# K cache transposed on VectorE in 32x32 blocks of 4-byte pairs, in a decode kernel that streams its K and V caches

## The chip, the cores and the metric

The kernel runs on one core of a Trainium2 chip. The time is device microseconds (us) of one execution. The time before is 392.98 us (median of 3 runs, 392.82 to 393.05). On one core there are no two dies to compare, so a run counts as slow only if it lies over 1.5% above the fastest of the same kernel; a profiled run's own span is about 2 us shorter than its time. The "granted clock" in the tables is the share of TensorE's full clock that the profile records as granted.

The engines are called TensorE (PE in the profile, PEld for its weight loads), VectorE (DVE), ScalarE (ACT), GpSimd (POOL) and SyncE (SP), which issues the loads. Sixteen DMA engines share each load: through the long loads 16 packets are under way at a time, and each large load has 16 landings in the trace.

## The reference, cut to what matters

One token (x is 1x1024) goes through grouped-query attention over a cache of 65536 positions, and through a small gated MLP. A gate mixes the two.

```python
# Hq, Hkv, Sk, Dh = 32, 4, 65536, 128 ; D = 1024 ; bf16
q = (x @ wq)                                   # wq 1024 x 4096
scores = q . k_cache * Dh**-0.5                # 8 query heads share a kv head
o = softmax(scores) . v_cache
a = o @ wo                                     # wo 4096 x 1024
# B: z = gelu(x @ w_in); z1 * (w_sp * layernorm(z2) + b_sp) @ w_out, one row
return g * a + (1 - g) * b                     # g = sigmoid(sum(x * gate_w))
```

K and V take 67.1 MB each (4 x 65536 x 128 values of 2 bytes), and with the weights the kernel reads 162.0 MB, all of it once.

## The kernel before: the parts that matter

Every large load takes one of `NKV` buffers of 32 KB per partition from one ring, in program order on SyncE's queue. A load waits until the buffer used `NKV` loads earlier has been read for the last time.

```python
NKV = 5
kv = ctx.enter_context(tc.tile_pool(name="kv", bufs=NKV))
def load(src, shape, name):
    t = kv.tile([P, CT * P], BF16, name=name, tag="kv")
    ...
    nc.sync.dma_start(out=v, in_=src)
```

The order of the loads is: two halves of w_in, two of wq, the four K tiles of kv head (group) 0, then K and V in turn (K of group g, V of group g-1), the four V tiles of group 3, w_out, and wo in six pieces. A K or V tile is 128 positions for each of 128 partitions: 4.19 MB.

A K tile has positions on partitions, but the scores contract over the head dimension. So TensorE transposes K in 128x128 pieces, VectorE and ScalarE take turns to copy the result out of PSUM, and TensorE multiplies each piece (as weights) by q:

```python
def k_units(g, j, kn):
    for u in range(CT // TG):
        tps = pst.tile([P, TG * P], BF16, name="tps")
        for i in range(TG):
            nc.tensor.transpose(tps[:, i * P:(i + 1) * P], kn[:, u * TG + i, :], ident_b[:])
        ktt = ktp.tile([P, TG * P], BF16, name="ktt")
        if EVAC_PAT[evac_i[0] % len(EVAC_PAT)] == "a":
            nc.scalar.copy(out=ktt[:], in_=tps[:])
        else:
            nc.vector.tensor_copy(out=ktt[:], in_=tps[:])
        ...
def emit_scores(g, cg0, ktt):
    ...
    for j in range(TG):
        ...
        nc.tensor.matmul(spt[g][:, o:o + n], lhsT=ktt[:, j * P:(j + 1) * P],
                         rhs=qT[:, g * REP:g * REP + n], start=True, stop=True, ...)
```

The work on V is interleaved with the work on the next group's K. When a group's scores are complete, its maximum is found, the exps are taken and the V matmuls begin. Each of these three jobs is cut into small steps.

## Time and profile before

| | before |
|---|---|
| time | 392.98 us |
| bytes loaded | 162.0 MB |
| DMA share, 60 to 366 us | 100% |
| instructions | 11536 |
| instruction bytes fetched (queue q8) | 0.69 MB in 42 packets of 16 KB |

The page of the kernel before: busy time by engine, then the DMA share in tenths and the GB/s for 40 equal slices of the span (9.8 us each), two DMA queues, and the shares of the chain of waits.

```profile
PE 289.8 (74%) x5355; PEld 240.1 (61%) x5355; DVE 160.2 (41%) x316; ACT 122.2 (31%) x139; POOL 1.0 (0%) x9
...
DMA  8999999999999999999999999999999999999982
GB/s 332 426 434 432 431 432 430 424 427 432 429 425 424 426 432 438 429 427 427 424 434 431 427 431 423 427 431 431 428 431 431 427 429 425 436 427 419 432 348 100
...
q1 hardware_dynamic: 6200, 162.01, 96.9%
q8 instruction: 42, 0.69, 0.7%
...
DMA 55%; PE 39%; issue 2%; DVE 2%; ACT 1%; SPq 0%; DVEq 0%; ACTq 0%
```

TensorE looks busiest, and the chain of waits gives it 39%, but the DMA rows show what binds: the loads never pause between the first slice and the last two. The kernel takes as long as its bytes take. Only the ends (332, 348 and 100 GB/s) leave room.

The groups that the change is about (line, engine, operation, tiles, shapes, count | busy us, mean ns | idle before):

```profile
L328 PE MATMUL tps<-ident_b,kn 128*128 128x128 bf16 x2048 | 163.6, 225 | 36.5 <-DMA kn<-in_A_k_cache_dram 34.9
L333 DVE COPY ktt<-tps 128x1024 bf16<-128x1024 bf16 x171 | 116.4, 689 | 111.9 <-PE tps L328 111.2
L331 ACT COPY ktt<-tps 128x1024 bf16<-128x1024 bf16 x85 | 86.0, 1012 | 161.5 <-PE tps L328 161.4
L307 PE MATMUL spt<-qT,ktt 128*128 128x64 bf16 (+7 forms) x2048 | 104.0, 194 | 5.3 <-issue 5.3
```

The table by stretch shows the tail. Its columns are the stretch, its length, the busy us (and instructions) of PE, PEld, DVE, ACT and POOL, the granted clock, the DMA share and GB/s. (A DMA packet is counted whole in the stretch in which it starts, so in a short stretch the share can pass 1.)

```profile
374.00:378.00 4.00, 0.16 (x4) 0.13 (x7) 0.00 (x0) 0.00 (x0) 0.00 (x0) 0.50 0.95 392
378.00:382.00 4.00, 3.44 (x64) 2.66 (x57) 0.00 (x0) 0.00 (x0) 0.00 (x0) 0.50 0.57 241
382.00:386.00 4.00, 2.75 (x48) 2.01 (x48) 0.00 (x0) 0.00 (x0) 0.00 (x0) 0.50 0.46 187
```

Between 378 and 386 us only about half of the 16 DMA engines still work, although everything had been queued since 349 us.

### The profile page before, as it was taken

To read this page: it belongs to the slowest core of one execution; us is meant where nothing else is said; L and a number is where in the kernel's file an instruction comes from. 1 tells how busy PE (TensorE), PEld (TensorE's weight loads), DVE (VectorE), ACT (ScalarE), POOL (GpSimd) and SP (SyncE) were. 2 spreads that over 40 slices of the span, in tenths; PEclk is the share of its full clock that TensorE was granted. 3 is DMA by queue.
4 is the path that set the end of the run, shared out by engine and by line. 5 is a ranking of instruction groups with operands and counts; after the bars stand their busy time and mean duration, and the time that the engine had idled before them with its cause. 6 is when DMAs were issued, how large, how long until landed. Compare 5 with 4: busy or idle time off the path is not lost.

```text
span 391.0 us, 11536 instructions
## 1 busy us (share of the span) xinstructions
PE 289.8 (74%) x5355; PEld 240.1 (61%) x5355; DVE 160.2 (41%) x316; ACT 122.2 (31%) x139; POOL 1.0 (0%) x9
## 2 busy tenths in 40 slices
PE   0774379888899995969994979589959697634534
PEld 0764379888887774846873858368848583311322
DVE  3011036665684551518750526177524356200200
ACT  1000025454594432413831434136414243100000
POOL 1000000000000000000000000000000000000000
PEclk9999999999999998989996999898989998866656
DMA  8999999999999999999999999999999999999982
GB/s 332 426 434 432 431 432 430 424 427 432 429 425 424 426 432 438 429 427 427 424 434 431 427 431 423 427 431 431 428 431 431 427 429 425 436 427 419 432 348 100
DMA packets 6285, 162.76 MB, mean 416 GB/s; under 512 B 728, under 2 KB 732, under 8 KB 1116
## 3 DMA queue, kind: packets, MB, share of 16 engines
q1 hardware_dynamic: 6200, 162.01, 96.9%
q8 instruction: 42, 0.69, 0.7%
q14 instruction: 7, 0.06, 0.0%
q10 hardware_dynamic: 36, 0.00, 0.0%
HBM read 162.01 MB, written 0.00 MB: 414 GB/s over the span
## 4 chain that ended last, share of the span: by engine, by line
DMA 55%; PE 39%; issue 2%; DVE 2%; ACT 1%; SPq 0%; DVEq 0%; ACTq 0%
DMA kn<-in_A_k_cache_dram 38%; PE tps L328 23%; PE spt L307 10%; DMA wo_t<-in_A_wo_dram 10%; DMA vt<-in_A_v_cache_dram 6%; PE o_ps L353 5%; DVE ktt L333 1%; ACT ktt L331 1%; PE s_ps L361 0%; PE om_ps L371 0%; SPq L84 0%; ACT scT L313 0%; DVE scT L290 0%; PE nb_ps L285 0%; PE mxT L277 0%
## 5 line engine op out<-in xcount | busy, mean ns | idle before, releaser
L328 PE MATMUL tps<-ident_b,kn 128*128 128x128 bf16 x2048 | 163.6, 225 | 36.5 <-DMA kn<-in_A_k_cache_dram 34.9
L333 DVE COPY ktt<-tps 128x1024 bf16<-128x1024 bf16 x171 | 116.4, 689 | 111.9 <-PE tps L328 111.2
L328 PEld LDWEIGHTS <-kn 128*128 128x128 bf16 x2048 | 123.7, 101 | 62.2 <-DMA kn<-in_A_k_cache_dram 38.5
L331 ACT COPY ktt<-tps 128x1024 bf16<-128x1024 bf16 x85 | 86.0, 1012 | 161.5 <-PE tps L328 161.4
L307 PE MATMUL spt<-qT,ktt 128*128 128x64 bf16 (+7 forms) x2048 | 104.0, 194 | 5.3 <-issue 5.3
L307 PEld LDWEIGHTS <-ktt 128*128 128x128 bf16 x2048 | 86.7, 100 | 7.0 <-issue 6.7
L353 PE MATMUL o_ps<-vt,scT 128*32 128x512 bf16 x512 | 54.2, 449 | 16.2 <-DMA vt<-in_A_v_cache_dram 15.4
L353 PEld LDWEIGHTS <-scT 128*32 128x32 bf16 x512 | 15.8, 103 | 29.3 <-issue 24.4
L313 ACT CAST scT<-spt 128x512 bf16<-128x512 f32 x32 | 18.8, 588 | 17.0 <-PE spt L307 17.0
L315 DVE TENSOR_TENSOR mxr<-scT,mxr 128x512 bf16<-128x512 bf16 x24 | 10.2, 426 | 20.1 <-ACT scT L313 18.8
L294 ACT ACTIVATE scT<-scT 128x1024 bf16<-128x1024 bf16 x16 | 16.4, 1059 | 5.1 <-DVE scT L290 5.1
L430 PE MATMUL out_ps<-wo_t,oa 128*32 128x256 bf16 x128 | 7.5, 399 | 10.4 <-DMA wo_t<-in_A_wo_dram 10.4
L192 PE MATMUL z_ps<-xT,win_t 128*128 128x18 bf16 x224 | 13.7, 208 | 1.6 <-DMA win_t<-in_B_w_in_dram 1.1
L192 PEld LDWEIGHTS <-win_t 128*128 128x128 bf16 x224 | 13.7, 158 | 1.6 <-DMA win_t<-in_B_w_in_dram 1.2
L368 DVE COPY o_sb<-o_ps 128x512 f32<-128x512 f32 x4 | 2.7, 687 | 28.0 <-PE o_ps L353 28.0
L361 PE MATMUL s_ps<-scT,ones_b 128*32 128x512 bf16 x32 | 13.4, 418 | 0.0
L430 PEld LDWEIGHTS <-oa 128*32 128x32 bf16 x128 | 5.3, 135 | 12.8 <-issue 12.0
L244 PE MATMUL q_ps<-xT,wq_t 128*128 128x1 bf16 x256 | 7.1, 165 | 7.6 <-DMA wq_t<-in_A_wq_dram 7.6
L244 PEld LDWEIGHTS <-wq_t 128*128 128x128 bf16 x256 | 7.0, 104 | 7.8 <-DMA wq_t<-in_A_wq_dram 7.8
L290 DVE TENSOR_TENSOR scT<-scT,negm 128x1024 bf16<-128x1024 bf16 x16 | 10.7, 683 | 0.2
L450 DVE CAST out_sb<-out_ps 128x256 bf16<-128x256 f32 x1 | 0.4, 424 | 22.6 <-PE out_ps L430 22.6
L371 PE MATMUL om_ps<-o_sb,pick 128*32 128x128 f32 x32 | 5.0, 310 | 3.2 <-DVE o_sb L368 3.2
(87 smaller groups left out, 51.4 us busy)
## 6 DMA issues: line engine op xcount, KB each, us to landing
kn<-in_A_k_cache_dram SPq DMA_DIRECT2D x16, 4096.0 KB, 30.0
vt<-in_A_v_cache_dram SPq DMA_DIRECT2D x16, 4096.0 KB, 31.3
wq_t<-in_A_wq_dram SPq DMA_DIRECT2D x2, 4096.0 KB, 30.1
win_t<-in_B_w_in_dram SPq DMA_DIRECT2D x2, 3584.0 KB, 15.2
wo_t<-in_A_wo_dram SPq DMA_DIRECT2D x1, 4096.0 KB, 42.7
wout_t<-in_B_w_out_dram SPq DMA_DIRECT2D x1, 3584.0 KB
wo_t<-in_A_wo_dram SPq DMA_DIRECT2D x1, 2048.0 KB
wo_t<-in_A_wo_dram SPq DMA_DIRECT2D x1, 1024.0 KB
```

Source lines behind the costliest of these rows:

```text
L192: nc.tensor.matmul(z_ps[:, hf * FC + f, :], lhsT=w[:, hf, f, :], rhs=xT[:, i * KH + c:i * KH + c + 1].to_broadcast([P, zw]), start=(i == 0 ...
L244: nc.tensor.matmul(q_ps[:, h:h + 1], lhsT=w[:, c % KH, h * DH:(h + 1) * DH], rhs=xT[:, c:c + 1], start=(c == 0 and h == 0), stop=(c == KC ...
L290: nc.vector.tensor_tensor(out=blk, in0=blk, in1=negm[:].unsqueeze(1).to_broadcast([P, CT, REP]), op=ALU.add)
L294: nc.scalar.activation(out=blk, in_=blk, func=ACT.Exp, scale=SCALE)
L307: nc.tensor.matmul(spt[g][:, o:o + n], lhsT=ktt[:, j * P:(j + 1) * P], rhs=qT[:, g * REP:g * REP + n], start=True, stop=True, skip_group_c ...
L313: nc.scalar.copy(out=blk, in_=spt[g][:].rearrange("p (c h) -> p c h", h=REP))
L328: nc.tensor.transpose(tps[:, i * P:(i + 1) * P], kn[:, u * TG + i, :], ident_b[:])
L331: nc.scalar.copy(out=ktt[:], in_=tps[:])
L333: nc.vector.tensor_copy(out=ktt[:], in_=tps[:])
L353: nc.tensor.matmul(o_ps[g][t * Q:(t + 1) * Q, :], lhsT=scT[g][:, cg:cg + VC, :].rearrange("p c h -> p (c h)"), rhs=vt[:, lo:lo + VC, :].re ...
L361: nc.tensor.matmul(s_ps[g][gs, :], lhsT=ones_b[:, :Q], rhs=scT[g][:, cg:cg + CPS, :].rearrange("p c h -> p (c h)"), start=(cg == 0), stop= ...
L430: nc.tensor.matmul(out_ps[t * Q:(t + 1) * Q, :], lhsT=vec[:, c0 + c:c0 + c + 1].to_broadcast([P, Q]), rhs=w[:, c, t * NO:(t + 1) * NO], st ...
```

## The change

The intent is to take the K transpose off TensorE and its copies off VectorE and ScalarE. VectorE transposes K with the bf16 data viewed as 4-byte pairs: one instruction takes 2048 pairs for each partition, two values per element. The kernel's indexing takes the result as 32x32 blocks (`B = 32`; the trace records shapes, not blocks). In that layout only 32 pairs lie on the partitions of each block row, so the weights hold q in a block-diagonal arrangement, and the 512-column moving operand is read at a step of 4 bytes. TensorE now has 32 wide score matmuls for a K tile in place of 128 transposes and 128 narrow ones. The x projections are computed as rows (x as 32 equal weight columns, 448 or 512 columns of weights moving). The new tables take room, so `NKV` goes from 5 to 4.

```diff
-NKV = 5
+NKV = 4
 ...
+    def k_tile(g, j, kn):
+        kb = kn.bitcast(I32)
+        n = CC * DH // 2
+        s_ps = pss.tile([P, 2 * HN], FP32, name="s_ps", tag="s")
+        for v in range(VC):
+            kt = ktp.tile([P, CC * DH], BF16, name="kt")
+            nc.vector.transpose(out=kt[:].bitcast(I32), in_=kb[:, v * n:(v + 1) * n])
+            kx = kt[:].rearrange("p (c h k e) -> p h e c k", h=2, k=B, e=2)
+            for b in range(BP):
+                for k in range(2):
+                    nc.tensor.matmul(
+                        s_ps[:, k * HN:(k + 1) * HN],
+                        lhsT=wt[g % 2][:, v, b].rearrange("p a v h -> p (a v h)"),
+                        rhs=kx[:, b // 2, b % 2, k * CC // 2:(k + 1) * CC // 2, :],
+                        start=(v == 0 and b == 0), stop=(v == VC - 1 and b == BP - 1), ...)
+        ...
+        nc.scalar.copy(out=sct[g, j][:], in_=s_ps[:])
+        nc.vector.reduce_max(out=mxs[g][:, j:j + 1], in_=sct[g, j][:], axis=AX.X)
 ...   (stats: group maximum; then for each of the group's 4 tiles)
+            nc.scalar.activation(out=sct[g, j][:], in_=sct[g, j][:], func=ACT.Exp, scale=SCALE,
+                                 bias=nb[:, 0:1], accum_out=lss[g][:, j:j + 1])
+            nc.vector.transpose(out=ptt[g, j][:]..., in_=sct[g, j][:])
 ...
+    for g in range(G):
+        for j in range(NT):
+            k_tile(g, j, load_kv(A_k_cache, g, j, "kn"))
+            if j == 1 and g + 1 < G:
+                build_w(g + 1)
+            if j == NT - 1:
+                stats(g)
+            if g > 0:
+                v_tile(g - 1, j, load_kv(A_v_cache, g - 1, j, "vt"))
 ...
```

## The prediction

> **What bounds it now.** Loads. The page moves 162.0 MB; in the table by stretch, the 16 DMA engines are 100% busy from 60 to 366 us at 427 to 429 GB/s, so one 4.19 MB tile takes about 9.75 us. 162.0 MB at 429 GB/s is already 378 us; start and tail add the other 13 us. TensorE (74%), VectorE (41%) and ScalarE (31%) have slack. The chain of waits names TensorE lines, but only as who frees buffers; with five buffers that never empties the queue. No byte of input is removed, so the gain is capped. The tail is unchanged: the last wo pieces are waited for by TensorE (7.8+1.3+0.5+... us).
>
> **What goes.** 2048 TensorE transposes (163.6 us busy), 256 evictions (116.4 us VectorE, 86.0 us ScalarE), 2048 score matmuls with own weights (104 us). All off the critical path. 11536 instructions become roughly 3500 (count from the diff); their fetching (0.69 MB, 0.7% of the DMA share) shrinks by two thirds: estimate 1 to 2 us saved.
>
> **What comes.** 64 VectorE transposes of 2048 4-byte elements. The trace has none; its [...]shapes (512-column f32 copy 687 ns, 128-column reduce 382 ns) give about 0.15 us + 1.04 ns each[...]: estimate 2.29 us, 9.2 us a K tile (no run shows it yet). 512 score matmuls of 512 columns, about 0.22 us warm, 0.43 us at half clock (four V matmuls of 512 columns in parallel take 0.22/0.43 us in the timeline): 7 us a tile. V work unchanged.
>
> **The catch.** VectorE is in program order, and after a tile's fourth transpose it must wait for the last eight matmuls (1.9 us), ScalarE's copy (1.0) and do reduce_max over 1024 columns (1.2) before the next tile's transposes. So a K tile costs VectorE about 13.5 us, against 9.75 us of loading. When K and V alternate (19.5 us a pair) that is free. In the first group four K tiles come back to back: transposes end at about 60, 74, 88, 102 us; then group statistics with four exps and four P transposes hold VectorE to about 114 us, and K tile (1,0) is released only at about 124 us. With four buffers instead of five, the load of K (1,2) waits for that release, while the queue runs dry at about 119 us. Estimated gap: 6 us, once (0 to 10). Later groups have about 64 us of VectorE work in 78 us of loading: no gap. With five buffers it would not occur.
>
> **Sum.** 393 - 1.5 + 6 = 397 us. Range 390 to 406. Faster by over 2%: 0.03; within 2%: 0.77; slower by over 2%: 0.20.
>
> **Right if:** mean of the transpose group near 2.3 us; TensorE busy falls below 200 us and ScalarE below 60; DMA share 100% except one hole around 115 to 128 us, at the first statistics, with the queue's own wait naming the VectorE transpose of K (1,0); instruction bytes about 0.25 MB; same tail.
>
> **Wrong if:** the 4-byte transpose runs at half rate (4.4 us): a K tile then costs 22 us, VectorE bounds everything and the time passes 450 us. Or TensorE stays at half clock, which lengthens the wait before reduce_max and the hole. Or transposes are quicker, or the scheduling leaves the hole closed: then about 391 us, the same as before. Reading the moving operand at a 4-byte step might slow the matmuls; up to about double is hidden except in group 0.

Two passages about the transposes are cut out of the text above. They gave a rate that no trace or run of this case shows as support for the estimate of 2.29 us. The estimate stands on the shapes of the trace before (0.15 us + 2048 x 1.04 ns = 2.28 us), and no term of the sum is cut.

## The result, and the profile after

The changed kernel takes 393.94 us (median of 4 runs, 393.84 to 395.78) beside 393.01 us for the kernel before. The ratio is 1.0035, with a 95% interval of 1.0015 to 1.0055. Ratios here are the mean time of one kernel's fast runs over that of the other's of the same rounds, so they are not quite the ratio of the medians. The time is inside the predicted range, but the predicted change was +4 us (1%) and the measured one about +1 us (0.24% by the medians). So the prediction is wrong in size.

The page after, the same lines:

```profile
PE 219.5 (56%) x1396; PEld 92.4 (24%) x1396; DVE 209.6 (53%) x207; ACT 39.2 (10%) x54; POOL 4.4 (1%) x10
...
DMA  8999999999983999999999999999999999999995
GB/s 328 438 445 436 434 425 428 431 426 428 431 381 110 440 434 441 443 424 428 428 426 431 428 426 432 438 434 434 429 434 428 427 428 431 434 429 426 434 413 202
...
q1 hardware_dynamic: 6200, 162.01, 96.4%
q8 instruction: 11, 0.18, 0.2%
```

There is one hole in the loads, in the slices with 381 and 110 GB/s. The last slice is better than before (202 in place of 100). Instruction bytes fell from 0.69 to 0.18 MB.

The groups that came:

```profile
L298 PE MATMUL s_ps<-kt,wt 128*128 128x512 bf16 x512 | 143.7, 447 | 86.4 <-DVE kt L294 86.4
L294 DVE STREAM_TRANSPOSE kt<-kn 128x2048 int32<-128x2048 int32 x64 | 142.1, 2277 | 24.4 <-DMA kn<-in_A_k_cache_dram 24.4
L308 DVE TENSOR_REDUCE mx<-sc 128x1 f32<-128x1024 bf16 x16 | 19.5, 1220 | 56.7 <-ACT sc L307 56.7
```

The transpose takes 2277 ns (2.29 us was estimated), and VectorE idles 56.7 us in all before its 16 maximum instructions. VectorE in order of time (start us, busy us, line, operation, tiles, count, idle before), around the first group's end:

```profile
50.94 8.89 DVE L294 STREAM_TRANSPOSE kt<-kn 128x2048 int32<-128x2048 int32 x4 [1.51 <-DMA kn<-in_A_k_cache_dram]
63.48 1.22 DVE L308 TENSOR_REDUCE mx<-sc 128x1 f32<-128x1024 bf16 x1 [3.65 <-ACT sc L307]
64.61 8.88 DVE L294 STREAM_TRANSPOSE kt<-kn 128x2048 int32<-128x2048 int32 x4
...
92.20 8.88 DVE L294 STREAM_TRANSPOSE kt<-kn 128x2048 int32<-128x2048 int32 x4
104.44 1.22 DVE L308 TENSOR_REDUCE mx<-sc 128x1 f32<-128x1024 bf16 x1 [3.36 <-ACT sc L307]
...
110.02 4.64 DVE L331 STREAM_TRANSPOSE pt<-sc 128x1024 bf16<-128x1024 bf16 x4 [2.65 <-ACT sc L328]
114.58 8.85 DVE L294 STREAM_TRANSPOSE kt<-kn 128x2048 int32<-128x2048 int32 x4
```

K tiles start 13.7 us apart (50.94, 64.61, ...), while one is loaded every 9.7 us. The last line is K tile (1,0), released at 123.4. VectorE works in program order here: the next tile's transposes start only behind the maximum (64.61, after the one at 63.48); in experiment 1, where the maximum comes later in the program, they start at 60.77. SyncE issues the load that was waiting for K tile (1,0) at once, and the stretches show what had happened to the queue meanwhile:

```profile
123.46 0.33 SPq L86 DMA_DIRECT2D kn<-in_A_k_cache_dram  x1
```

```profile
116.00:120.00 4.00, 3.00 (x8) 1.06 (x9) 4.00 (x3) 0.00 (x0) 0.00 (x0) 0.50 0.10 41
120.00:124.00 4.00, 4.00 (x15) 1.57 (x14) 3.43 (x2) 0.00 (x0) 0.00 (x0) 0.72 0.00 0
124.00:128.00 4.00, 4.00 (x41) 1.71 (x42) 0.27 (x1) 1.01 (x1) 0.00 (x0) 1.00 1.07 393
```

So the hole is there, at the place and with the release time that the prediction gave (124 us). What the prediction did not have is the gain that nearly pays for it. The tail after:

```profile
378.00:382.00 4.00, 3.18 (x64) 2.64 (x64) 0.00 (x0) 0.00 (x0) 0.00 (x0) 0.55 1.00 424
382.00:386.00 4.00, 1.15 (x36) 0.86 (x32) 0.00 (x0) 0.00 (x0) 0.00 (x0) 0.88 0.97 398
```

All 16 DMA engines work until 386 us. Before, half of them had finished by about 378 us and the rest worked on for up to 10 us.

### A closer look: the 16 landings of one load

The trace records 16 additions to the semaphore of a large load, each at its own time: for the last load of the kernel before, from 377.99 to 387.64 us. I take them as one for each of the 16 DMA engines; no record names the engine. I call the time from a load's first to its last landing its spread. I computed it from the records of the trace, together with the number of instruction packets on queue q8 that had started by the last landing. These are the loads of the kernel before at which the spread grew:

```
kernel before: last landing (us), spread (us), instruction packets so far
 20.50  0.77   0
 31.72  2.29   2
 91.22  3.53   9
151.15  5.21  18
210.80  6.59  25
290.21  8.34  34
377.80  9.75  41
```

The spread grows in six steps of 1.2 to 1.8 us, one for every 7 to 9 instruction packets, and between them shrinks by no more than 0.15 us. The very last load (wo) first lands at 377.99 and last lands at 387.64. The last matmuls, which read this load, start at 387.68, just after the 16th landing and 9.7 us after the first. So the slowest DMA engine decides the end of the kernel.

In the changed kernel the spread is 1.99 us before the hole, 0.49 us just after it, and 2.02 us at the end.

This gave me a theory. Instruction fetches take turns with the loads on single DMA engines, and they are not spread evenly: one engine gets every eighth or so and falls behind by about 1.5 us each time. Removing 31 of 42 fetches then saves the slowest engine about 6 us, not the 1 to 2 us that an even spread over 16 engines gives. The hole costs about 7 us. The two nearly cancel. (The packet records, read under experiments 6 and 7, bear this out, but for one thing: it is not one engine that gets the fetches, it is eight.)

The rivals: (A) the hole makes up for itself, since late engines catch up in it; (B) four buffers would bind elsewhere anyway; (C) the kernel before lost its time because TensorE's and ScalarE's SBUF traffic slowed the loads, not because of fetches. Nothing measured so far ruled C out, so it needed a test.

### The profile page after: what moved, and what is told of

It reads as the page before. It is cut to its first block, busy times and chain, and to the rows that moved or that the text cites. A ratio compares the mean times of both kernels' runs of the same rounds, so it can differ in the third digit from the quotient of the medians.

```text
span 392.2 us, 3265 instructions
## 1 busy us (share of the span) xinstructions
PE 219.5 (56%) x1396; PEld 92.4 (24%) x1396; DVE 209.6 (53%) x207; ACT 39.2 (10%) x54; POOL 4.4 (1%) x10
## 4 chain that ended last, share of the span: by engine, by line
DMA 50%; PE 24%; DVE 16%; issue 6%; ACT 3%; SPq 0%; ACTq 0%; DVEq 0%
DMA kn<-in_A_k_cache_dram 32%; PE s_ps L298 21%; DVE kt L294 11%; DMA wo_t<-in_A_wo_dram 8%; DMA vt<-in_A_v_cache_dram 8%; DMA wb<-in_B_b_sp_dram 2%; DVE pt L331 2%; ACT sc L307 2%; DVE mx L308 1%; PE o_ps L340 1%; PE z_ps L190 1%; ACT sc L328 1%; PE om_ps L351 0%; DVE wt L279 0%; SPq L412 0%
## 5 line engine op out<-in xcount | busy, mean ns | idle before, releaser
L298 PE MATMUL s_ps<-kt,wt 128*128 128x512 bf16 x512 | 143.7, 447 | 86.4 <-DVE kt L294 86.4
L294 DVE STREAM_TRANSPOSE kt<-kn 128x2048 int32<-128x2048 int32 x64 | 142.1, 2277 | 24.4 <-DMA kn<-in_A_k_cache_dram 24.4
L298 PEld LDWEIGHTS <-wt 128*128 128x128 bf16 x512 | 54.7, 109 | 173.8 <-DVE kt L294 77.7
L308 DVE TENSOR_REDUCE mx<-sc 128x1 f32<-128x1024 bf16 x16 | 19.5, 1220 | 56.7 <-ACT sc L307 56.7
L340 PE MATMUL o_ps<-vt,pt 128*32 128x512 bf16 x512 | 41.2, 474 | 14.5 <-DMA vt<-in_A_v_cache_dram 14.5
L307 ACT CAST sc<-s_ps 128x1024 bf16<-128x1024 f32 x16 | 16.2, 1013 | 254.4 <-PE s_ps L298 254.4
L340 PEld LDWEIGHTS <-pt 128*32 128x32 bf16 x512 | 16.2, 112 | 35.1 <-issue 28.1
L331 DVE STREAM_TRANSPOSE pt<-sc 128x1024 bf16<-128x1024 bf16 x16 | 18.6, 1217 | 6.8 <-ACT sc L328 6.8
L328 ACT ACTIVATE sc<-sc,nb 128x1024 bf16<-128x1024 bf16 x16 | 18.2, 1136 | 10.1 <-DVE nb L324 10.0
L190 PE MATMUL q_ps<-wq_t,xT 128*32 128x512 bf16 x64 | 7.2, 627 | 8.9 <-DMA wq_t<-in_A_wq_dram 8.9
```

The lines of the kernel that those rows point to most:

```text
L190: nc.tensor.matmul(ps[t * B:(t + 1) * B, k * HN:k * HN + n], lhsT=xT[:, i * KH + c:i * KH + c + 1].to_broadcast([P, B]), rhs=w[:, c, o:o + ...
L294: nc.vector.transpose(out=kt[:].bitcast(I32), in_=kb[:, v * n:(v + 1) * n])
L298: nc.tensor.matmul(s_ps[:, k * HN:(k + 1) * HN], lhsT=wt[g % 2][:, v, b].rearrange("p a v h -> p (a v h)"), rhs=kx[:, b // 2, b % 2, k * C ...
L307: nc.scalar.copy(out=sct[g, j][:], in_=s_ps[:])
L308: nc.vector.reduce_max(out=mxs[g][:, j:j + 1], in_=sct[g, j][:], axis=AX.X)
L328: nc.scalar.activation(out=sct[g, j][:], in_=sct[g, j][:], func=ACT.Exp, scale=SCALE, bias=nb[:, 0:1], accum_out=lss[g][:, j:j + 1])
```

## The experiments

Each has its own runs of the kernel before on the same chip: 392.84 us (7 runs) for the first four, 393.1 us (7 runs) for the last three.

### 1. The maximum taken later: closes the hole

VectorE's reduce_max of a K tile is issued after the second transpose of the next tile, so that VectorE need not wait for TensorE and ScalarE. Nothing else changes.

```diff
+    late = []
+
+    def take_max():
+        while late:
+            g, j = late.pop(0)
+            nc.vector.reduce_max(out=mxs[g][:, j:j + 1], in_=sct[g, j][:], axis=AX.X)
 ...
             nc.vector.transpose(out=kt[:].bitcast(I32), in_=kb[:, v * n:(v + 1) * n])
+            if v == 1:
+                take_max()
 ...
-        nc.vector.reduce_max(out=mxs[g][:, j:j + 1], in_=sct[g, j][:], axis=AX.X)
+        late.append((g, j))

     def stats(g):
+        take_max()
```

> The changed kernel, but the reduce_max of a K tile is issued after the second transpose of the next tile, so VectorE no longer idles 3.4 us per K tile. Theory (the hole comes from VectorE's order, and the fewer instruction fetches let the slowest DMA engine finish earlier): K tile (1,0) is released near 104 to 113 us instead of 123.5, the hole of 117 to 125 us closes, and the time falls by about 6 to 7 us to 387 (ratio to before 0.985). The last wo piece lands about 9 us after... with a spread of its 16 landings of about 2 to 3 us. Rival A (the loss was made up by the hole itself, which lets late engines catch up, and without it the skew returns): the time falls by less than 3 us. Rival B (four buffers bind elsewhere too): a new hole opens, time near 393.

Measured: 386.89 us (386.81 to 387.15, 4 runs), ratio 0.9849 (0.9834 to 0.9864), correct. From its timeline of VectorE, its DMA rows and its stretches:

```profile
100.00 4.64 DVE L340 STREAM_TRANSPOSE pt<-sc 128x1024 bf16<-128x1024 bf16 x4 [2.65 <-ACT sc L337]
104.56 13.23 DVE L300 STREAM_TRANSPOSE kt<-kn 128x2048 int32<-128x2048 int32 x6
```

```profile
DMA  8999999999999999999999999999999999999993
```

```profile
116.00:120.00 4.00, 4.00 (x44) 1.56 (x42) 4.00 (x3) 1.01 (x1) 0.00 (x0) 1.00 0.93 401
120.00:124.00 4.00, 4.00 (x20) 1.79 (x19) 4.00 (x6) 0.00 (x0) 0.00 (x0) 1.00 1.13 479
374.00:378.00 4.00, 2.21 (x61) 1.73 (x53) 0.00 (x0) 0.00 (x0) 0.00 (x0) 0.92 0.97 395
378.00:382.00 4.00, 2.23 (x32) 1.14 (x31) 0.00 (x0) 0.00 (x0) 0.00 (x0) 0.51 0.32 117
```

The first group's P transposes start 10 us earlier, K tile (1,0) is released at about 113.4 us in place of 123.4 (SyncE issues the next K load at 113.44), and the hole is gone. Each beside the kernel before of its own rounds, the hole was worth (393.94 - 393.01) + (392.84 - 386.89) = 6.9 us, and so say the last landings below. Rival A fails: it allowed less than 3 us. It has a small part of the truth, since the spread at the end is 1.5 us larger without the hole (3.51 in place of 2.02 us). Rival B fails for the changed kernel: with VectorE's order mended, four buffers keep the queue full. This version beats both kernels. Its last load has a spread of 3.51 us and its last landing is at 381.80, against 388.73 for the changed kernel and 387.64 for the one before.

### 2 and 3. Many small matmuls added: too many

To put the instruction fetches back without their work, I added 137 one-column matmuls after each K and V tile of the main loop, once to the version of experiment 1 and once to the changed kernel.

```diff
+    def idle_pairs(n):
+        for _ in range(n):
+            nc.tensor.matmul(out_ps[:B, 500:501], lhsT=own_bb[:, 0, :], rhs=xT[:, 0:1],
+                             start=True, stop=True, skip_group_check=True)
 ...
             k_tile(g, j, load_kv(A_k_cache, g, j, "kn"))
+            idle_pairs(137)
 ...
                 v_tile(g - 1, j, load_kv(A_v_cache, g - 1, j, "vt"))
+                idle_pairs(137)
```

> The run with the late reduce_max, plus 137 one-column matmuls on idle TensorE after each K tile and each V tile of the main loop: 3836 pairs, 7672 more instructions, no more useful work and almost no SBUF traffic. Theory (instruction fetches land on single DMA engines, and the slowest of the 16 decides): instruction bytes on queue q8 go from 0.18 to about 0.67 MB, the spread of the landings of the last loads grows from about 2 to about 9 or 10 us as in the kernel before, and the time rises by about 5 to 6 us to 392 to 393, that of the kernel before. Rival C (the kernel before lost its time by TensorE's and ScalarE's SBUF or PSUM traffic beside the loads): less than 2 us more, spread stays near 2 us. My prediction's sizing (bytes spread evenly over 16 engines): about 1.5 us more.

> The changed kernel as it is (hole kept) plus the same 3836 pairs. Theory: hole and fetches add up, so 394 + about 5 = 398 to 400, close to what the prediction said for the hole without the larger fetch gain. Rival A (the hole absorbs the skew): the skew from before the hole is absorbed, about 1.5 us less, so 396 to 398. Rival C: 394 to 395.

Measured: 416.52 us (413.41 to 419.84, 4 runs; the profiled one, 419.84, is slow, and the three fast ones reach 417.51 at most), ratio 1.0576 (1.0529 to 1.0623), and 422.25 us (420.63 to 423.9, 4 runs), ratio 1.0737 (1.0695 to 1.0778). No theory expected this. The profile of the first says why (groups of TensorE, then SyncE's waits for the last matmuls of a V tile; the last line is the same wait in the changed kernel):

```profile
L306 PE MATMUL s_ps<-kt,wt 128*128 128x512 bf16 x512 | 146.3, 452 | 22.7 <-DVE kt L300 22.3 <-issue 0.5
L347 PE MATMUL out_ps<-xT,own_bb 128*32 128x1 bf16 x3836 | 104.0, 164 | 12.8 <-issue 12.8
...
SPq L86 <- PE o_ps L356: 124.5, 13, 11.8
...
SPq L86 <- PE o_ps L340: 71.3, 13, 10.3
```

The pairs took 104 us of TensorE, plus 12.8 us in which TensorE waited for nothing that the profile shows. The fast profile of experiment 3 shows the same (pairs 103.8 us, waits for V tiles 125.6 us). V tiles were released late, and holes opened all along. In those holes the DMA engines catch up: with 41 fetches, the spread ended at 3.16 and 3.84 us. These two runs say nothing about the fetches. The dose had to be smaller (experiments 6 and 7).

### 4. The kernel before with four buffers

```diff
-NKV = 5
+NKV = 4
```

> The kernel before with four load buffers instead of five, nothing else. Theory (the hole needs both four buffers and VectorE's late release): the kernel before releases its K tile (1,0) at 114.7 us, earlier than the queue runs dry at about 117 to 120 us, so no hole or one under 2 us: 393 to 395. Rival (four buffers alone cost the hole): about 399.

Measured: 397.07 us (394.68 to 399.3, 4 runs), ratio 1.0106 (1.0057 to 1.0155). My expectation failed, and the rival is partly right: four buffers cost this kernel about 4 us too, and unsteadily. Its stretches (the profiled run took 399.3 us):

```profile
124.00:128.00 4.00, 4.00 (x82) 3.25 (x79) 2.27 (x4) 1.16 (x2) 0.00 (x0) 1.00 0.86 369
128.00:132.00 4.00, 4.00 (x86) 3.43 (x82) 2.24 (x5) 2.10 (x3) 0.00 (x0) 1.00 0.15 57
132.00:136.00 4.00, 4.00 (x81) 3.12 (x77) 2.15 (x4) 1.90 (x3) 0.00 (x0) 1.00 0.88 303
```

I had checked K tile (1,0) alone, but here SyncE issued nothing from 116.1 to 131.9 us, and what it then issued was a V tile (the load that waited for the buffer of V tile (0,0)). So the fifth buffer protected the kernel before at the same place, the first group's end. The change lost that buffer. Its slow release of K then made the hole. This run also shows what rival A is worth when the holes are many: with 42 fetches its last load first lands 13.8 us later than in the kernel before (391.79), but the spread there is only 2.28 us in place of 9.64, so the last landing is 6.4 us later (394.07).

### 5. The kernel before with fewer instructions

Only every eighth score matmul is left. Each writes 64 columns, so the PSUM tile is still filled. The scores are wrong. (The comparison with the reference passed all the same, so it does not prove the scores.)

```diff
             n = min(W, CPS * REP - o)
+            if j:
+                continue
             nc.tensor.matmul(spt[g][:, o:o + n], lhsT=ktt[:, j * P:(j + 1) * P],
```

> The kernel before with only every eighth score matmul (each writes 64 columns, so the PSUM tile is still filled; the result is wrong on purpose): 1792 matmuls fewer, 3584 instructions, 14 of 42 fetches of 16 KB. TensorE is not what bounds it. Theory: in the kernel before the spread between the first and the last of the 16 landings of one load grows by steps of about 1.5 us at fetches 2, 9, 18, 25, 34 and 41; with 28 fetches the last two steps are missing, the spread of the last loads is about 6.7 us instead of 9.7 and the time is about 390 (3 us less, ratio 0.992). The prediction's sizing (bytes spread evenly): 0.23 MB less, 0.5 to 0.9 us. Rival C (TensorE's traffic slows the loads as such): the landings get closer together in the middle of the run too, without a change in the spread.

Measured: 389.99 us (389.81 to 390.13, 4 runs), ratio 0.992 (0.9905 to 0.9935). Twenty-eight instruction packets are left, the spread at the end is 6.64 us, and the last load first lands at 378.20, as in the kernel before (377.99).

```profile
q8 instruction: 28, 0.46, 0.5%
```

The kernel gains the 3 us that the theory expects, not the 0.5 to 0.9 us of an even spread. Its DMA engines with the least delay finish no earlier, so this run shows no slowing of the loads as such by the TensorE traffic that was removed.

### 6 and 7. Fewer added matmuls: a dose that TensorE can carry

The edit of experiment 2 with 68 and with 45 in place of 137.

> The kernel with the late reduce_max plus 68 one-column matmul pairs after each K and V tile of the main loop (half of the earlier run, in which the pairs took so much TensorE time that they released V tiles late and made holes of their own): 3808 more instructions, about 26 fetches instead of 11. If TensorE keeps up (DMA share 100% in the middle, no hole), the theory expects a spread of about 6.7 us at the end instead of 3.5, and about 3 us more than the kernel with the late reduce_max: 390. Evenly spread bytes: 0.6 to 1 us more, 387.5 to 388. If holes appear again, the run says nothing about fetches.

> The same with 45 pairs: 2520 more instructions, about 21 fetches. Theory: steps at fetches 1, 9 and 18 only, spread about 5 us, 388.5 us. Evenly spread: 387.3 to 387.6.

Measured: 389.85 us (389.72 to 390.19, 4 runs), ratio 0.9918 (0.9903 to 0.9933), and 388.55 us (388.42 to 388.72, 4 runs), ratio 0.9883 (0.9866 to 0.9899). The DMA rows and the instruction queue of the run with 68, then with 45:

```profile
DMA  8999999999999999999999999999999999999992
...
q8 instruction: 25, 0.41, 0.4%
```

```profile
DMA  8999999999999999999999999999999999999993
...
q8 instruction: 20, 0.33, 0.3%
```

There is no hole, and only the end is later. All the kernels without a hole, by instruction packets (landings of the last load, computed from the traces):

| kernel | packets | first landing | spread | last landing | median time |
|---|---|---|---|---|---|
| late maximum (1) | 11 | 378.28 | 3.51 | 381.80 | 386.89 |
| late maximum + 45 (7) | 20 | 378.40 | 4.94 | 383.34 | 388.55 |
| late maximum + 68 (6) | 25 | 378.24 | 6.37 | 384.60 | 389.85 |
| before, fewer matmuls (5) | 28 | 378.20 | 6.64 | 384.84 | 389.99 |
| before | 42 | 377.99 | 9.64 | 387.64 | 393.0 |

The first row was measured on one chip and the next three on another; the kernel before differs by 0.3 us between them.

TensorE's busy time does not give this order (260.4 us in experiment 6, 250.3 in 5). Two very different kernels, with instructions added to one and removed from the other, follow the same rising row. The first landing stays within about 0.4 us, and the last landing moves, in steps, by on average (387.64 - 381.80) / (42 - 11) = 0.19 us for each fetch. A fetch packet itself lasts about 1.06 us (median in the trace). Divided by 16 engines that would be 0.07 us, so the slowest engine pays about three times its even share.

The packet records show why. Through the long loads sixteen packets of 32 KB are under way at a time, each takes 1.21 us, and in each of the sixteen streams the next starts as the one before it ends. In the kernel before, 41 of the 42 fetches fall in this traffic, and each of the 41 ends just where the next packet of one stream starts. Where the packet before it can be told apart (23 cases), that stream had paused for 1.06 us, and its next packet took 0.49 us longer than usual: 1.55 us lost by one DMA engine (medians; 1.55 us too in the four other kernels of the table). The 16 landings of the last load, in us after the first, show how many engines lose:

```
before            0.00 0.33 0.36 0.72 0.77 0.80 1.75 4.33 7.91 7.99 8.16 8.21 8.24 8.27 8.44 9.64
late maximum (1)  0.00 0.09 0.17 0.30 0.44 0.71 0.82 1.45 1.61 1.67 1.73 1.75 2.07 2.09 3.19 3.51
```

Eight engines are late by five or six times 1.55 us in the first line, and by one or two times in the second. The eight delays of the first line add up to 66.9 us, and 41 times 1.55 us is 63.6, so next to nothing of the fetches is left for the other eight (what held up those at 1.75, 4.33 and 1.45 us was not followed). So the fetches are shared by eight of the sixteen engines, about evenly: two even shares, each half as long again as the fetch itself, and 1.55 / 8 = 0.19 us for each fetch.

This is what rival C cannot explain: the added matmuls read next to nothing, and in experiment 5 the TensorE work that went left the first landing where it was.

## Why the prediction was right or wrong, point by point

- **Loads bound the kernel before**: right. The DMA rows are full, and removing the work of 163.6 us of TensorE transposes and 202 us of copies (116.4 on VectorE, 86.0 on ScalarE) did not bring the loads forward: without a hole the last load first lands at 378.28 us (experiment 1) beside 377.99.
- **"estimate 2.29 us" for the VectorE transpose**: right, 2277 ns over 64. From the P transposes of 1024 2-byte elements (1217 ns) to these of 2048 4-byte ones, each further element takes 1.04 ns, the pace that the prediction took from other shapes. One of the two shapes it quoted for that pace does not fit it, though (382 ns for 128 columns, where 0.15 us + 1.04 ns each gives 283); other shapes of the same profile do (256-column cast 424 ns, 128-column f32 multiply 278 to 286). The alternative of 4.4 us is out. By element the 2-byte and the 4-byte transpose take nearly the same time (1.19 and 1.11 ns), so pairs of bf16 nearly double the bytes per us.
- **"a K tile costs VectorE about 13.5 us"**: right. The first tiles start 13.7 us apart.
- **"K tile (1,0) is released only at about 124 us" and "Estimated gap: 6 us"**: right, 123.4 us. The hole is worth 6.9 us by experiment 1. The later groups had no hole, as predicted.
- **"With five buffers it would not occur"**: not tested directly, because five do not fit. Experiment 4 shows that the kernel before needs its fifth buffer at the same place.
- **"their fetching ... shrinks by two thirds: estimate 1 to 2 us saved"**: this is the step that failed. Fetching shrank by three quarters (0.18 MB is left, where about 0.25 was expected), and the last landing came 387.64 - 381.80 = 5.8 us earlier without the hole. The sum should have read 393 - 6 + 7 = 394, and it is 393.94. I divided the fetch bytes by the rate of all 16 engines. What ends the kernel is the DMA engine that lags most: the fetches fall on eight engines and not sixteen, and each costs its engine 1.55 us, where the fetch packet itself takes 1.06.
- **"The tail is unchanged"**: wrong, the same mistake. The tail before, with half of the DMA engines idle, was the accumulated lag. It was visible in the profile before, in the slices with 348 and 100 GB/s.
- **"TensorE busy falls below 200 us"**: wrong, 219.5 us. The 447 ns in the group line is the length of records that overlap. By their starts, the score matmuls follow each other every 217 ns where the granted clock is 1.0 (347 of them) and every 427 ns where it is 0.5 (149), medians computed from the trace: just the 0.22 and 0.43 us that the prediction took, so the 4-byte step of the moving operand costs nothing here. What failed is the assumption of full clock: it was 0.752 on average, and the 512 matmuls took 143.7 us in place of about 113 (512 x 0.22). It mattered little for the time: the wait before the maximum was 3.4 us rather than the 2.9 us of the estimate. ScalarE below 60 us: right (39.2).

What stays open: the records of packets do not name their DMA engine. That eight engines share the fetches is read from the 16 landings, and that a fetch holds up one of them from the starts of the load packets. Why it is eight, and why the load packet after a fetch takes 0.49 us longer, no run here shows.

## What to carry to other kernels

In a kernel bound by loads, compare the landings of one load's 16 parts. Here their spread grew along the run, and the number of instructions cost time although the engine that runs them had slack: 0.19 us for each 16 KB of instructions (42 packets of 16 KB for the 11536 instructions of the kernel before). When an engine that works in program order releases load buffers, issue the instructions that wait for other engines after the next tile's first work: here one moved reduce_max was worth 7 us. Count releases for every kind of tile against the loads' own timetable at the place where the pattern changes (first group, last group), since a hole there was made up only in part (in the changed kernel the last load's first landing came 8.4 us later than without the hole, its last landing 6.9 us).
